# Sliding-window attention and two gated layers on one core: when q and k are loaded, and who adds the mask in the first rounds

## The chip, the cores and the metric

The kernel runs on one core of a Trainium2 chip. The metric is the device time of one execution in microseconds (us). The engines are TensorE (PE: matmuls and, as PEld, the loads of their weights), VectorE (DVE), ScalarE (ACT), GpSimd (POOL) and SyncE (SP), whose queue issues every transfer of this kernel.

## The reference

Three layers follow one another. q, k and v are (4, 8, 576, 64); the second and third layer have width 512, and inner width 1024.

```python
scores = scale * np.matmul(q, k.transpose(0, 1, 3, 2))
mask = (rel >= 0) & (rel < 64)                 # rel = query position - key position
scores = np.where(mask, scores, -1000000000.0)
attn = exp(scores - max) / (sum + 1e-09);  x = attn @ v
h = np.maximum(x @ w_in, 0.0)
conv_out = sum over k of conv_w[k] * hp[:, k:k + S, :]          # 3 taps along the sequence
x = (h * gate) @ w_out                                          # gate = 1 / (1 + exp(-conv_out))
h = np.maximum(x @ moe2_w_in, 0.0);  u, v = halves of h
v_s = einsum('ts,bsd->btd', w_spatial, layernorm(v)) + b_spatial
out = (u * v_s) @ moe2_w_out
```

## The kernel before, in words

**Attention.** The 576 positions of a batch are 9 blocks of 64. Because the window is 64 wide, a block of queries needs two blocks of keys. A round takes two blocks in turn over all batches, so there are 18 rounds (`rec_round`), and rounds 0 to 3 are of batch 0, round 4 is half of batch 0 and half of batch 1, round 9 is the first of batch 2. In a round TensorE makes scores for 8 heads in 32 small matmuls (line 537) into two PSUM tiles `s` of 4 heads each, of which the pool has two. For each head VectorE adds the mask, negates and scales, and takes the minimum in one fused pass, written to SBUF as `sm` (line 553). ScalarE takes the exponential with that minimum as bias and sums it (line 562). Then come the division (line 578 or 582), a transpose on TensorE (592), a copy (285) and the product with v (618), whose result is split into a high and a low part as `xc`, the input of the next layer.

**Loads of q, k and v.** Batch 0 is read in five tiles (`rec_load_first`, line 454) and transposed on TensorE (489). Batches 1 to 3 are read by `rec_load_qk` (line 466), eight transfers a batch (four of q, four of k) straight into `qT` and `kT` in pieces of 32 elements, and put in order by VectorE's 32x32 transpose (503). Batches 0 and 2 share one buffer, 1 and 3 the other. v comes in windows of 128 positions (`rec_load_v`, line 477) into three buffers.

**The conv layer.** x is cut into 8 chunks of 288 positions. For a chunk, `rec_g1` makes 8 column groups of h (lines 710 to 712), followed by relu, three taps and the gate on ScalarE and VectorE; `rec_g2` makes y (777 to 779) one chunk later and stores it to DRAM (802). The weights arrive as 64-bit numbers in two `raw` buffers (676 for w_in, 638 for w_out and moe2_w_in), are turned to float32 by VectorE and ScalarE (650 to 665) and split into high and low parts (`split`); all matmuls of the two gated layers are done in three such parts. The first chunk needs rounds 0 to 2, the second rounds 3 and 4.

**The last layer** begins when all chunks are done (`rec_v`, `rec_u`, `rec_sp`, `rec_o`).

**The order.** Nothing is issued in the order in which it is written down. Each step is an operation of `Plan` with a rank (its due time, from the constants in `PLAN`), its dependencies, its buffers and one planned duration per engine that may run it. `Plan.emit` plays this through with one queue per engine (T, V, A, P, D for SP): an operation becomes ready when what it depends on is done, the ready operation of lowest rank is taken when its engine is free, and the list that results is the order in which each engine gets its instructions. The times are the planner's own; on the chip an engine works through its list in order, waiting only for data and buffers. A queue with nothing more urgent that is ready takes the next ready operation at once, whatever its rank. Where several engines may run a step, each one's planned duration is multiplied by a weight (`BIAS1` before the planner's time TE1, `BIAS2` until TE2, `BIAS` after that; 1 for ScalarE).

Of the kernel before, what the change touches and what calls it, by code (L numbers as in the profile page):

```python
# [13 lines left out]
ACTF = mybir.ActivationFunctionType  # L14
ALU = mybir.AluOpType
PSUM = bass.MemoryType.PSUM
NEG = -8.0e9
BIG = 3.0e38
EXP_SHIFT = 2.0 ** -112

PLAN = {
    "BP": 2.148,
    "BP1": 0.05,
    "BP2": 15.503,
    "BV": 0.462,
    "BV1": 0.753,
    "BV2": 4.229,
    "CS": 2.842,
    "CW": 4.897,
    "CWL": -1.999,  # L30
    "DC": 1.72,
    "G2": 7.85,
    "LAT": 0.209,
    "LD": 0.07,
    "LEAD": -0.623,
    "PORT": 1.851,
    "QK": 0.74,
    "QL": -0.201,
    "QL1": -1.324,
    "QV": -0.054,  # L40
    "RD": 5.317,
    "RS": 1.023,
    "SW": 4.365,
    "TA": -1.408,
    "TE1": 1.82,
    "TE2": 574.465,
    "TL": 1.208,
    "TR": 0.83,
    "VL": -0.489,
    "W2": 13.512,  # L50
    "WI": 1.844,
    "WIS": -0.265,
    "WO": -0.591,
    "WOS": 2.232,
}
LAT = PLAN["LAT"]
HOLD, ISSUE = 0.25, 0.45
BIAS = {"V": PLAN["BV"], "P": PLAN["BP"]}
BIAS1 = {"V": PLAN["BV1"], "P": PLAN["BP1"]}
BIAS2 = {"V": PLAN["BV2"], "P": PLAN["BP2"]}  # L60
# [24 lines left out]
class Plan:  # L85
# [4 lines left out]
    def __init__(self):  # L90
        self.rows, self.bufs, self.ops = {}, [], []
        self.writer, self.readers = {}, {}
        self.port, self.issues = set(), {}

    def buf(self, key, n, make):
        return Buf(self, key, n, make)

    def op(self, rank, engs, fn, r=(), w=(), b=(), after=(), port=False, issues=1):


        i = len(self.ops)
        if port:
            self.port.add(i)
        self.issues[i] = issues
        deps = set(after)
# [12 lines left out]
        for x in b:  # L118
            x.users.append(i)
        deps.discard(i)  # L120
        self.ops.append([rank, engs, fn, deps, b])
        return i

    def emit(self):
# [18 lines left out]
        events = []  # L143
        for i in range(n):
            if not left[i]:
                heapq.heappush(events, (0.0, 0, i))
        port_free = wire = 0.0
        order = []
        t = 0.0
        while events:  # L150
            t = events[0][0]
            while events and events[0][0] <= t + 1e-9:
                _, kind, i = heapq.heappop(events)
                if kind == 0:
                    rank, opt = ops[i][0], ops[i][1]
                    e = min(
                        opt,
                        key=lambda k: (
                            max(free[k], t) + opt[k] * bias(k, t) + sum(ops[j][1][k] for r_, j in ready[k] if r_ < rank), k
                        ),  # L160
                    ) if len(opt) > 1 else next(iter(opt))
                    heapq.heappush(ready[e], (rank, i))
                elif kind == 1:
                    for j in out[i]:
                        left[j] -= 1
                        if not left[j]:
                            heapq.heappush(events, (t, 0, j))
            for e in engs:
                while ready[e] and free[e] <= t + 1e-9:
                    if e == "V" and free["P"] > t + HOLD:  # L170
# [9 lines left out]
                    if e == "V" and i in self.port:  # L180
                        begin = max(t, free["P"])
                        port_free = begin + cost
                    elif e == "P":
                        begin = max(t, port_free)
                    elif e == "D":
                        free[e] = t + ISSUE * self.issues[i]
                        wire = max(wire, free[e]) + cost
                        begin, lat = wire - cost, 2.0
                    if e != "D":
# [24 lines left out]
def tile_attention_convglu_spatial(  # L214
# [44 lines left out]
    op = plan.op  # L259
    mm = nc.tensor.matmul  # L260
    ident = const.tile([P, P], F, name="ident")
    masks = [const.tile([P, P], F, name=f"mask{j}") for j in range(3)]
# [92 lines left out]
    def setup_masks(e):  # L355


        for mk_, first in zip(masks, ((False, False), (True, False), (False, True))):
# [14 lines left out]

    op(-9.0, {"P": 0.8}, setup_ident, w=["ident"])
    op(-9.0, {"A": 1.6}, setup_table, w=["zero1"])
    op(-8.0, {"P": 3.0}, setup_masks, w=["masks"])

    def setup_ones(e):
        nc.gpsimd.memset(zero2, 0.0)
# [80 lines left out]
    def rec_load_qk(b, rank):  # L460

        for nm, src, dst in (("q", q, qT), ("k", k, kT)):
            for g in range(4):
                def ld(e, src=src, dst=dst, g=g):
                    part = src[b, 4 * (g // 2):4 * (g // 2) + 4, :, 32 * (g % 2):32 * (g % 2) + 32]
                    nc.sync.dma_start(
                        out=dst[b]()[32 * g:32 * g + 32].rearrange("p h (u c) -> p (h u) c", c=32),
                        in_=part.rearrange("h (u t) c -> t (h u) c", t=32),
                    )
                op(rank + 0.1 * g, {"D": 1.8}, ld, w=[(nm, b, "ld", g)], b=[dst[b]])  # L470

    def rec_load_v(b, w, rank):
        a = mk(at, [P, H, D], F, "vw", "vw", 3)
# [35 lines left out]
    def x_pieces(blocks):  # L509
# [9 lines left out]
            c0 += n  # L519
        return out_  # L520

    x_keys = {qc: [] for qc in range(NQ)}

    def rec_round(p, rank):
# [4 lines left out]
        sm = [mk(at, [P, HP, P], F, "sm", "sm", 4) for _ in range(2)]  # L529
        st = mk(at, [P, 3, 2, HP], F, "st", "st", 3)  # L530

        def mm_s(e):
# [9 lines left out]
        op(  # L542
            rank, {"T": 1.1}, mm_s,
            r=[("q", b, i) for b, i in blocks] + [("k", b, k0 + o) for (b, _), k0 in zip(blocks, k0s) for o in range(2)],
            w=[("s", p, h) for h in range(2)], b=pss + [qT[b] for b in bs] + [kT[b] for b in bs],
        )
        firsts = [i == 0 for _, i in blocks]
        mask = masks[1 if firsts[0] else 2 if firsts[1] else 0]
# [10 lines left out]
        def ex(h):  # L559
            def f(e):  # L560
                for hp in range(HP):
                    nc.scalar.activation(  # L562
                        out=sm[h]()[:, hp, :], in_=sm[h]()[:, hp, :], func=ACTF.Exp, scale=-1.0,
                        bias=st()[:, 0, h, hp:hp + 1], accum_out=st()[:, 1, h, hp:hp + 1],
                    )
            return f
# [25 lines left out]
                    nc.tensor.transpose(psp[h]()[:, hp, :], sm[h]()[:, hp, :], ident)  # L592
            return f
        for h in range(2):
            op(rank + 1 * rs + 0.1 * h, {"V": 1.46}, mx(h), r=[("s", p, h), "masks"], w=[("sm", p, h)], b=[pss[h], sm[h], st])
            op(rank + 2 * rs + 0.1 * h, {"A": 1.9}, ex(h), r=[("sm", p, h)], w=[("ex", p, h)], b=[sm[h], st])
# [602 lines left out]
```

## Time and profile before

| | |
|---|---|
| median of 3 runs | 548.48 us (547.16 to 550.54) |
| profiled execution | 549.49 us, span 547.7 us |
| mean granted TensorE clock | 0.956 |
| PE, PEld busy | 508.4 us (93%), 472.7 us (86%) |
| DVE, ACT, POOL busy | 345.1 us (63%), 324.4 us (59%), 4.3 us (1%) |
| transfers | 68.05 MB in 131993 packets, 105740 of them under 512 B |

Busy shares over the whole span hide that the work has stages with different limits; the rows further down are read by stretch. Matmuls overlap in their pipeline, so the mean duration of one is longer than the distance from one to the next.

### The profile page before, as it was taken

To read this page: it belongs to the slowest core of one execution; us is meant where nothing else is said; L and a number is where in the kernel's file an instruction comes from. 1 tells how busy PE (TensorE), PEld (TensorE's weight loads), DVE (VectorE), ACT (ScalarE), POOL (GpSimd) and SP (SyncE) were. 2 spreads that over 40 slices of the span, in tenths; PEclk is the share of its full clock that TensorE was granted. 3 is DMA by queue.
4 is the path that set the end of the run, shared out by engine and by line. 5 is a ranking of instruction groups with operands and counts; after the bars stand their busy time and mean duration, and the time that the engine had idled before them with its cause. 6 is when DMAs were issued, how large, how long until landed. Compare 5 with 4: busy or idle time off the path is not lost.

```text
span 547.7 us, 11063 instructions
## 1 busy us (share of the span) xinstructions
PE 508.4 (93%) x4198; PEld 472.7 (86%) x4198; DVE 345.1 (63%) x1045; ACT 324.4 (59%) x920; POOL 4.3 (1%) x34
## 2 busy tenths in 40 slices
PE   5745967999999999999999999999999999999997
PEld 5634857899988999999999998898899889988996
DVE  2547768999977989777676634986506740572160
ACT  4875879988959899678785524653322442233221
POOL 3000000000000000000000000000000000000000
PEclk9765788999998999999999999999999999999999
DMA  9999997655996746224216682560105011202003
GB/s 181 173 145 178 147 184 209 190 162 148 208 151 183 226 117 181 68 61 143 69 45 196 215 303 93 166 208 4 59 20 172 1 63 35 87 1 78 1 0 97
DMA packets 131993, 68.05 MB, mean 124 GB/s; under 512 B 105740, under 2 KB 118308, under 8 KB 131940
## 3 DMA queue, kind: packets, MB, share of 16 engines
q1 hardware_dynamic: 131940, 67.35, 51.5%
q8 instruction: 33, 0.54, 0.4%
q14 instruction: 20, 0.16, 0.1%
HBM read 48.98 MB, written 18.35 MB: 123 GB/s over the span
## 4 chain that ended last, share of the span: by engine, by line
PE 80%; DMA 7%; SPq 5%; ACT 3%; DVE 3%; issue 1%; ACTq 0%
PE y L777 6%; PE h L710 5%; PE h L711 5%; PE y L779 5%; PE h L712 5%; PE y L778 5%; DMA vw<-in_v_dram 3%; PE pv L618 3%; PE sps L1053 3%; PE sps L1055 3%; PE sps L1054 3%; PE ops L1108 3%; PE vps L930 3%; PE ops L1107 3%; PE ops L1106 3%; PE vps L929 3%
## 5 line engine op out<-in xcount | busy, mean ns | idle before, releaser
L710 PE MATMUL h<-xc,wi 128*128 128x290 f32 x256 | 79.7, 311 | 2.1 <-ACT hs L301 2.1
L777 PE MATMUL y<-g,wo 128*128 128x288 f32 x256 | 78.4, 306 | 0.8 <-DVE ys L795 0.8
L712 PE MATMUL h<-xc,wi 128*128 128x290 f32 x256 | 77.2, 301 | 0.0
L711 PE MATMUL h<-xc,wi 128*128 128x290 f32 x256 | 77.1, 301 | 0.0
L779 PE MATMUL y<-g,wo 128*128 128x288 f32 x256 | 76.1, 297 | 0.0
L778 PE MATMUL y<-g,wo 128*128 128x288 f32 x256 | 75.9, 296 | 0.0
L738 DVE SCALAR_TENSOR_TENSOR cv<-hs,cw,cv 128x288 f32<-128x288 f32 x128 | 64.5, 512 | 15.9 <-ACT cv L733 14.7
L1067 DVE TENSOR_TENSOR gr<-sps,bb 128x288 f32<-128x288 f32 x32 | 14.5, 454 | 71.9 <-PE sps L1059 71.9
L562 ACT ACTIVATE sm<-sm,st 128x128 f32<-128x128 f32 x144 | 55.7, 391 | 2.2 <-DVE st L553 2.2
L710 PEld LDWEIGHTS h<-xc,wi 128*128 128x128 f32 x256 | 49.9, 195 | 3.8 <-ACT hs L301 2.9
L777 PEld LDWEIGHTS y<-g,wo 128*128 128x128 f32 x256 | 48.5, 189 | 2.7 <-DVE ys L795 1.1
L711 PEld LDWEIGHTS h<-xc,wi 128*128 128x128 f32 x256 | 49.9, 195 | 0.0
L712 PEld LDWEIGHTS h<-xc,wi 128*128 128x128 f32 x256 | 49.6, 194 | 0.1
L779 PEld LDWEIGHTS y<-g,wo 128*128 128x128 f32 x256 | 48.7, 190 | 0.0
L778 PEld LDWEIGHTS y<-g,wo 128*128 128x128 f32 x256 | 48.6, 190 | 0.0
L578 ACT ACTIVATE sm<-sm,st 128x128 f32<-128x128 f32 x132 | 41.1, 393 | 1.0 <-DVE st L571 0.8
L285 ACT ACTIVATE gd<-gr 128x288 fp32r<-128x288 f32 (+1 forms) x32 | 13.4, 418 | 47.2 <-DVE gr L1070 47.2
L553 DVE CUSTOM_DVE_ANT_0 sm<-s,mask 128x128 f32<-128x128 f32 x144 | 32.3, 286 | 10.9 <-PE s L537 10.9
L989 PE MATMUL ups<-yt,w2i 128*128 128x288 f32 x128 | 37.9, 296 | 0.0
L990 PE MATMUL ups<-yt,w2i 128*128 128x288 f32 x128 | 37.9, 296 | 0.0
L991 PE MATMUL ups<-yt,w2i 128*128 128x288 f32 x128 | 37.9, 296 | 0.0
L618 PE MATMUL pv<-pts,vw 128*64 128x64 f32 x576 | 25.8, 250 | 12.5 <-DMA vw<-in_v_dram 9.4
(147 smaller groups left out, 1240.5 us busy)
## 6 DMA issues: line engine op xcount, KB each, us to landing
yd<-ys SPq DMA_DIRECT2D x32, 288.0 KB, 3.0
yt<-yd SPq DMA_DIRECT2D x32, 288.0 KB, 4.3
vw<-in_v_dram SPq DMA_DIRECT2D x32, 256.0 KB, 4.0
raw<-in_moe_w_out_dram SPq DMA_DIRECT2D x12, 512.0 KB, 3.9
raw<-in_moe_w_in_dram SPq DMA_DIRECT2D x16, 256.0 KB, 5.3
raw<-in_moe_w_in_dram SPq DMA_DIRECT2D x8, 512.0 KB, 5.0
w2i<-w2d SPq DMA_DIRECT2D x8, 512.0 KB, 6.1
out_dram<-osb SPq DMA_DIRECT2D x15, 256.0 KB, 2.0
```

The costliest lines, as they stand in the source:

```text
L562: nc.scalar.activation(out=sm[h]()[:, hp, :], in_=sm[h]()[:, hp, :], func=ACTF.Exp, scale=-1.0, bias=st()[:, 0, h, hp:hp + 1], accum_out=s ...
L578: nc.scalar.activation(out=sm[h]()[:, hp, :], in_=sm[h]()[:, hp, :], func=ACTF.Copy, scale=st()[:, 2, h, hp:hp + 1])
L618: mm(psv()[h * W:h * W + W, hp, j * W:j * W + W], vas[j]()[:, hp + HP * h, :], pts[h]()[:, hp, j * W:j * W + W], start=True, stop=True,)
L710: mm(hps(), wh, xh, start=(kk == 0), stop=False)
L711: mm(hps(), wh, xl, start=False, stop=False)
L712: mm(hps(), wl, xh, start=False, stop=(kk == KD - 1))
L738: return lambda e: nc.vector.scalar_tensor_tensor(out=cv(), in0=h[:, o + j:o + j + CH], scalar=cw[:, j, f:f + 1], in1=cv(), op0=ALU.mult, ...
L777: mm(yps(), wt[:, 0], gt[:, 0, :], start=(kk == 0), stop=False)
L778: mm(yps(), wt[:, 0], gt[:, 1, :], start=False, stop=False)
L779: mm(yps(), wt[:, 1], gt[:, 0, :], start=False, stop=(kk == KF - 1))
L989: mm(ups(), wt[:, 0], yt[b][0]()[:, kk, o], start=(kk == 0), stop=False)
L990: mm(ups(), wt[:, 0], yt[b][1]()[:, kk, o], start=False, stop=False)
```

## The change

It has two parts and a new set of constants.

First, `Plan.op` takes a time `at`. An operation does not become ready in the planner before it, even when all it depends on is done. Only `rec_load_qk` gives one: its own rank, which is the due time of the batch's first round less `QL`. In the same place the planner's SP queue is changed: after an issue it is not free again until the planned backlog of transfers is under `DEPTH` = 6 us, the planned issue costs 0.5 and not 0.45 us, and such a load 2.0 and not 1.8 us. No instruction of the chip is added by this; only the order of the lists changes.

Second, in rounds 0 to 5 (`EARLY = 6`) TensorE writes the mask into each of the two `s` tiles by one matmul of an identity with the mask, repeated for four heads (512 columns, float32r), and adds the scores to it. VectorE then takes one maximum over the four heads and multiplies the four results by -scale; ScalarE's exponential reads the scores from PSUM and not from `sm`, so an `s` tile stays in use until the exponential is done. For this the masks are made in a float32 tile by GpSimd and copied by VectorE into float32r tiles, with a copy of the identity; the mask's value becomes -(2 ** 33).

All but a few constants of `PLAN` change too, so that ranks, and with them the whole list, are different. By the formulas of the kernel the due time of the loads of batch 1 goes from 14.4 to 20.3 us, of batch 2 from 95.0 to 84.2, of batch 3 from 152.3 to 128.1; of the eight w_in loads from 0.4 to 18.3 before to 9.9 to 16.1; of the eight w_out loads from 25.4 to 41.1 before to 21.7 to 33.2. In `BIAS2` VectorE's weight goes from 4.229 to 4.057, GpSimd's from 15.503 to 3.837; `TE2` from 574.465 to 358.933, and beyond it VectorE's weight is 7.261 and GpSimd's 0.925.

```diff
-NEG = -8.0e9
+NEG = -(2.0 ** 33)
...
-    "BP": 2.148,
-    "BP1": 0.05,
-    "BP2": 15.503,
-    "BV": 0.462,
-    "BV1": 0.753,
-    "BV2": 4.229,
...
+    "BP": 0.925,
+    "BP1": 2.459,
+    "BP2": 3.837,
+    "BV": 7.261,
+    "BV1": 0.378,
+    "BV2": 4.057,
...
-    "QL": -0.201,
+    "QL": -1.296,
...
-    "TE2": 574.465,
+    "TE2": 358.933,
...
-HOLD, ISSUE = 0.25, 0.45
+HOLD, ISSUE, DEPTH = 0.25, 0.5, 6.0
...
-                heapq.heappush(events, (0.0, 0, i))
+                heapq.heappush(events, (max(0.0, self.at.get(i, 0.0)), 0, i))
...
-                            heapq.heappush(events, (t, 0, j))
+                            heapq.heappush(events, (max(t, self.at.get(j, 0.0)), 0, j))
...
-                        free[e] = t + ISSUE * self.issues[i]
+                        free[e] = max(t + ISSUE * self.issues[i], wire - DEPTH)
...
+    def put_masks(e):
+        for j in range(3):
+            nc.vector.tensor_copy(out=masks_r[j], in_=mf()[:, j])
+        nc.vector.tensor_copy(out=ident_r, in_=ident)
...
-                op(rank + 0.1 * g, {"D": 1.8}, ld, w=[(nm, b, "ld", g)], b=[dst[b]])
+                op(rank + 0.1 * g, {"D": 2.0}, ld, w=[(nm, b, "ld", g)], b=[dst[b]], at=rank)
...
+    EARLY = 6
...
+        early = p < EARLY
+
         def mm_s(e):
+            if early:
+                for h in range(2):
+                    mm(pss[h](), ident_r, masks_r[which].unsqueeze(1).to_broadcast([P, HP, P]), start=True, stop=False)
             for hp in range(HP):
                 for h in range(2):
                     for j, (b, i) in enumerate(blocks):
                         rows = slice(h * W, h * W + W)
                         mm(
                             pss[h]()[j * W:j * W + W, hp, :], qT[b]()[rows, hp, i * W:i * W + W],
-                            kT[b]()[rows, hp, k0s[j] * W:k0s[j] * W + P], start=True, stop=True,
+                            kT[b]()[rows, hp, k0s[j] * W:k0s[j] * W + P], start=not early,
+                            stop=not early or hp == HP - 1,
                         )
...
         def mx(h):
             def f(e):
+                if early:
+                    m = st()[:, 0, h]
+                    nc.vector.tensor_reduce(out=m, in_=pss[h](), axis=mybir.AxisListType.X, op=ALU.max)
+                    nc.vector.tensor_scalar(out=m, in0=m, scalar1=-scale, scalar2=None, op0=ALU.mult)
+                    return
...
+                    src = pss[h] if early else sm[h]
                     nc.scalar.activation(
-                        out=sm[h]()[:, hp, :], in_=sm[h]()[:, hp, :], func=ACTF.Exp, scale=-1.0,
+                        out=sm[h]()[:, hp, :], in_=src()[:, hp, :], func=ACTF.Exp, scale=scale if early else -1.0,
...
+            op(
+                rank + 2 * rs + 0.1 * h, {"A": 1.75 if early else 1.9}, ex(h),
+                r=[("sm", p, h)], w=[("ex", p, h)], b=[sm[h], st] + [pss[h]] * early,
+            )
```

## Rows read from the trace of the kernel before

**Rows 1.** Busy us (x instructions) of each engine by stretch, granted clock, DMA share

```profile
13.00:57.00 44.00, 26.13 (x287) 20.55 (x288) 25.84 (x110) 32.95 (x115) 0.00 (x0) 0.62 1.13 168
57.00:96.00 39.00, 31.25 (x319) 29.22 (x319) 30.79 (x93) 33.16 (x101) 0.00 (x0) 0.86 1.00 180
96.00:120.00 24.00, 21.91 (x204) 20.45 (x199) 23.58 (x50) 21.42 (x50) 0.00 (x0) 1.00 0.61 174
120.00:200.00 80.00, 78.05 (x829) 74.35 (x829) 69.83 (x235) 66.09 (x213) 0.00 (x0) 0.98 0.81 178
...
120.00:547.70 427.70, 421.72 (x3335) 395.59 (x3334) 261.67 (x772) 232.04 (x645) 0.00 (x0) 1.00 0.39 110
```

**Rows 2.** The chain that ended last: start us, us, what

```profile
46.68 6.63 DMA vw<-in_v_dram
...
78.58 6.65 DMA vw<-in_v_dram
```

**Rows 3.** The SP queue in order of time: start us, us, what it issued

```profile
17.66 1.41 SPq L466 DMA_DIRECT2D qT<-in_q_dram  x1
...
27.11 2.92 SPq L676 DMA_DIRECT2D raw<-in_moe_w_in_dram  x2
...
39.04 2.85 SPq L454 DMA_DIRECT2D qk<-in_q_dram  x2
...
52.34 0.60 SPq L466 DMA_DIRECT2D qT<-in_q_dram  x1
...
66.13 2.58 SPq L676 DMA_DIRECT2D raw<-in_moe_w_in_dram  x2
...
70.04 2.80 SPq L466 DMA_DIRECT2D qT<-in_q_dram  x1
...
75.72 2.17 SPq L676 DMA_DIRECT2D raw<-in_moe_w_in_dram  x2
...
97.91 7.70 SPq L638 DMA_DIRECT2D raw<-in_moe_w_out_dram  x3
...
139.79 0.41 SPq L466 DMA_DIRECT2D qT<-in_q_dram  x1
```

**Rows 4.** TensorE in order of time: scores of rounds 2, 3, 4, 9

```profile
22.19 1.10 PE L537 MATMUL s<-kT,qT 64*64 64x128 f32 x32
...
25.77 1.20 PE L537 MATMUL s<-kT,qT 64*64 64x128 f32 x32 [1.89 <-ACT kT L285]
...
47.78 1.99 PE L537 MATMUL s<-kT,qT 64*64 64x128 f32 x32
...
57.15 0.59 PE L710 MATMUL h<-xc,wi 128*128 128x290 f32 x1
...
151.58 1.10 PE L537 MATMUL s<-kT,qT 64*64 64x128 f32 x32
```

**Rows 5.** Groups by line and form, 0 to 120 us: count, busy us, mean ns

```profile
L562 ACT ACTIVATE sm<-sm,st 128x128 f32<-128x128 f32 x56 | 21.6, 392 | 1.6 <-DVE st L553 1.6
...
L710 PE MATMUL h<-xc,wi 128*128 128x290 f32 x68 | 22.6, 332 | 2.1 <-ACT hs L301 2.1
...
L553 DVE CUSTOM_DVE_ANT_0 sm<-s,mask 128x128 f32<-128x128 f32 x56 | 12.6, 286 | 7.3 <-PE s L537 7.3
...
L285 ACT ACTIVATE pts<-pt 128x512 f32<-128x512 f32 x14 | 8.4, 598 | 0.5 <-PE pt L592 0.4
...
L553 DVE DVE_READ_ACCUMULATOR2_ANT st<- 128x1 f32 x56 | 4.7, 84 | 0.0
...
L285 ACT ACTIVATE wi<-wt 128x512 fp32r<-128x512 f32 x7 | 4.4, 631 | 0.0
...
L306 DVE TENSOR_TENSOR xc<-pv,xc 128x512 fp32r<-128x512 f32 x4 | 2.7, 680 | 0.2 <-ACT xc L285 0.2
...
L570 DVE TENSOR_SCALAR st<-st 128x4 f32<-128x4 f32 x6 | 1.0, 165 | 2.2 <-ACT sm L562 2.2
...
masks.py:199 POOL TENSOR_SCALAR_AFFINE_SELECT ident<-ident 128x128 f32<-128x128 f32 x1 | 0.3, 292 | 0.1
```

More of the change, by code (lines that the diff above doesn't have):

```diff
@@ L21 @@
 PLAN = {
-    "BP": 2.148,
-    "BP1": 0.05,
-    "BP2": 15.503,
-    "BV": 0.462,
-    "BV1": 0.753,
-    "BV2": 4.229,
-    "CS": 2.842,
-    "CW": 4.897,
-    "CWL": -1.999,
+    "BP": 0.925,
[4 more added lines that the diff above has]
+    "BV2": 4.057,
+    "CS": 2.298,
+    "CW": 1.037,
+    "CWL": -1.498,
     "DC": 1.72,
-    "G2": 7.85,
+    "G2": 0.435,
     "LAT": 0.209,
[L34 to L37, printed above, removed]
-    "QL": -0.201,
[L39 to L45, printed above, removed]
-    "TE2": 574.465,
[L47 to L54, printed above, removed]
+    "LD": 2.893,
+    "LEAD": 2.263,
+    "PORT": 4.777,
+    "QK": 0.786,
+    "QL": -1.296,
+    "QL1": -1.611,
+    "QV": 1.559,
+    "RD": 1.978,
+    "RS": 1.79,
+    "SW": 0.744,
+    "TA": -1.335,
+    "TE1": 2.007,
+    "TE2": 358.933,
+    "TL": -0.795,
+    "TR": 5.148,
+    "VL": -10.672,
+    "W2": 15.278,
+    "WI": 0.476,
+    "WIS": -1.114,
+    "WO": 4.681,
+    "WOS": 1.641,
 }
 LAT = PLAN["LAT"]
-HOLD, ISSUE = 0.25, 0.45
+HOLD, ISSUE, DEPTH = 0.25, 0.5, 6.0
 BIAS = {"V": PLAN["BV"], "P": PLAN["BP"]}
@@ L92, in __init__, with op @@
         self.writer, self.readers = {}, {}
-        self.port, self.issues = set(), {}
+        self.port, self.issues, self.at = set(), {}, {}
     def buf(self, key, n, make):
         return Buf(self, key, n, make)
-    def op(self, rank, engs, fn, r=(), w=(), b=(), after=(), port=False, issues=1):
+    def op(self, rank, engs, fn, r=(), w=(), b=(), after=(), port=False, issues=1, at=0.0):
         i = len(self.ops)
@@ L104, in op @@
         self.issues[i] = issues
+        self.at[i] = at
         deps = set(after)
@@ L261, in tile_attention_convglu_spatial @@
     ident = const.tile([P, P], F, name="ident")
-    masks = [const.tile([P, P], F, name=f"mask{j}") for j in range(3)]
+    masks_r = [const.tile([P, P], R, name=f"mask{j}") for j in range(3)]
+    masks = [x_.bitcast(F) for x_ in masks_r]
+    ident_r = const.tile([P, P], R, name="ident_r")
     cw = const.tile([P, 3, KF], F, name="cw")
@@ L355, in setup_masks @@
     def setup_masks(e):
-        for mk_, first in zip(masks, ((False, False), (True, False), (False, True))):
+        for mk_, first in zip([mf()[:, j] for j in range(3)], ((False, False), (True, False), (False, True))):
             for h in range(2):
@@ L375, in tile_attention_convglu_spatial @@
     op(-9.0, {"A": 1.6}, setup_table, w=["zero1"])
-    op(-8.0, {"P": 3.0}, setup_masks, w=["masks"])
+    mf = mk(p2, [P, 3, P], F, "wu", "mf", 1)
+    def put_masks(e):
+        for j in range(3):
+            nc.vector.tensor_copy(out=masks_r[j], in_=mf()[:, j])
+        nc.vector.tensor_copy(out=ident_r, in_=ident)
+    op(-8.0, {"P": 3.0}, setup_masks, w=["masks_f"], b=[mf])
+    op(-7.0, {"V": 0.6}, put_masks, r=["masks_f", "ident"], w=["masks", "masks_r"], b=[mf])
     def setup_ones(e):
@@ L530, in rec_round @@
         st = mk(at, [P, 3, 2, HP], F, "st", "st", 3)
+        firsts = [i == 0 for _, i in blocks]
+        which = 1 if firsts[0] else 2 if firsts[1] else 0
+        mask = masks[which]
+        early = p < EARLY
         def mm_s(e):
+            if early:
+                for h in range(2):
+                    mm(pss[h](), ident_r, masks_r[which].unsqueeze(1).to_broadcast([P, HP, P]), start=True, stop=False)
             for hp in range(HP):
@@ L542, in rec_round @@
         op(
-            rank, {"T": 1.1}, mm_s,
-            r=[("q", b, i) for b, i in blocks] + [("k", b, k0 + o) for (b, _), k0 in zip(blocks, k0s) for o in range(2)],
+            rank, {"T": 1.75 if early else 1.1}, mm_s,
+            r=["masks_r"] * early + [("q", b, i) for b, i in blocks] + [("k", b, k0 + o) for (b, _), k0 in zip(blocks, k0s) for o in range(2)],
             w=[("s", p, h) for h in range(2)], b=pss + [qT[b] for b in bs] + [kT[b] for b in bs],
         )
-        firsts = [i == 0 for _, i in blocks]
-        mask = masks[1 if firsts[0] else 2 if firsts[1] else 0]
         def mx(h):
             def f(e):
+                if early:
[3 more added lines that the diff above has]
+                    return
                 for hp in range(HP):
@@ L594, in rec_round @@
         for h in range(2):
-            op(rank + 1 * rs + 0.1 * h, {"V": 1.46}, mx(h), r=[("s", p, h), "masks"], w=[("sm", p, h)], b=[pss[h], sm[h], st])
-            op(rank + 2 * rs + 0.1 * h, {"A": 1.9}, ex(h), r=[("sm", p, h)], w=[("ex", p, h)], b=[sm[h], st])
+            kept = [sm[h], st] if not early else [st]
+            op(
+                rank + 1 * rs + 0.1 * h, {"V": 0.85 if early else 1.46}, mx(h),
+                r=[("s", p, h), "masks"], w=[("sm", p, h)], b=[pss[h]] + kept,
+            )
+            op(
+                rank + 2 * rs + 0.1 * h, {"A": 1.75 if early else 1.9}, ex(h),
+                r=[("sm", p, h)], w=[("ex", p, h)], b=[sm[h], st] + [pss[h]] * early,
+            )
             if p < first_rounds:
```

## The prediction

> **What bounds the kernel now.** I read the busy time by stretch first, then the chain of work that ended last, then the queue that issues the transfers, then TensorE's order of work, then the costs by line. From 120 us to the end TensorE is busy for 421.72 of 427.70 us [rows 1]: that part is matmul, and nothing in the change makes a matmul there shorter. Before 120 us it is another kernel. TensorE is busy for 26.13 of 44, 31.25 of 39 and 21.91 of 24 us, so 27.7 us of idle time lie between 13 and 120 us, and its granted clock is 0.62 in the first of these stretches and 0.86 in the second: some of the busy time is half speed besides [rows 1]. VectorE and ScalarE are not full either: 80.2 and 87.5 us of 107. What is full is the transfer side, with a share of 1.13 and 1.00 up to 96 us and 0.61 after it [rows 1]. (A share over 1 counts packets that overlap on one engine.)
>
> The chain says the same by name: three waits for a window of v, the first and the last of them 6.6 us long, stand on it between 46 and 86 us [rows 2]. The SP queue shows why these windows are late. The eight loads of q and k of batch 1 (line 466) begin to issue at 17.66 us, and with one pair of w_in halves between them they hold the queue until 39.04 us; only then comes the last tile of batch 0, and behind it more w_in and the windows of v that the chain waits for. From 52.34 to 75.72 us the same happens with the eight loads of batch 2 [rows 3]. Who needs them? The blocks are taken two at a time, nine a batch, so batch 1 is first read by round 4, whose scores start at 47.78 us, and batch 2 by round 9, at 151.58 us: that batch is fetched 75 us too early, while the first conv matmul has waited until 57.15 us for x [rows 4].
>
> **The loads of q and k.** By the queue's own times one batch costs 39.04 - 17.66 - 2.92 = 18.5 us and the other (66.13 - 52.34) + (75.72 - 70.04) = 19.5 us [rows 3]. The change keeps a ready load out of the planner's list until its due time, and lets the planner run at most 6 us ahead of its wire. Due times follow from the constants: batch 1 at 20.3 us and batch 2 at 84.2 us, both in the planner's clock (before: 14.4 and 95.0, but only as ranks, so an idle queue took them at once). All eight w_in conversions are now due by 16.1 and the first three windows of v by 14.5. So I expect in the SP queue: the tiles of batch 0, three windows of v, three or four w_in, then batch 1 mixed with the rest of w_in, then w_out, and batch 2 only behind w_out. Batch 1 is still moved before 120 us, so its move brings the first rounds forward and saves no transfer time; batch 2's 19.5 us leave the crowded stretch altogether. The last w_out issues, at 97.91 us and 7.70 us after it [rows 3], would then come near 85 us. That is the transfer side's limit on the gain: **19.5 us**.
>
> The second limit is VectorE and ScalarE, which convert the weights, and run the softmax and the gate. Between 13 and 120 us they carry 167.7 us of work, 78% of 214; from 96 to 120 us, where no load is missing, 45.0 of 48, which is 94% [rows 1]. If the same work, less 9.2 us (next part), is packed at 94%, the 107 us become 158.5/2/0.94 = 84.3: a gain of 22.7. I don't expect that from the first us on: three rounds of attention run through both engines in turn before any conv work exists. At 86%, midway between the two, it is 158.5/2/0.86 = 92.2 us, a gain of **14.8 us**; at 80% it is 99.1, a gain of 7.9. I take 14.8, under both limits.
>
> What the move costs: batch 2 now occupies SP for its 19.5 us somewhere past 85 us, in front of stores of y, the split weights' stores and later windows of v, all on that queue. Batch 3 does exactly that in the trace, from 139.79 us [rows 3], and the stretch from 120 to 200 us around it lost 80 - 78.05 = 2 us of TensorE [rows 1]. I take **1 us**, bounds 0 and 2. The loads are not too late: round 9 is due no earlier than about 135 us in any of these cases.
>
> **Mask and maximum in rounds 0 to 5.** Removed from VectorE for each half round: four fused mask-and-minimum passes of 286 ns and their four accumulator reads of 84 ns, 1.48 us. Added: one maximum over 128x512 from PSUM and a 4-element scaling. The trace has no such maximum. The nearest row is the 128x512 subtraction that reads PSUM, 680 ns; half of it bounds it from below, four fused passes (1.14 us) from above. The scaling is the 4-element row, 165 ns [rows 5]. With 0.68 + 0.165 = 0.85 us a half round saves 0.63, twelve of them **7.6 us** of VectorE (2.1 to 11.7). ScalarE's 48 exponentials read PSUM and not SBUF: a 128x512 copy takes 598 ns from PSUM and 631 from SBUF [rows 5], so 33 ns each, **1.6 us** in all, and nothing if that does not carry over. These are the 9.2 us above; by themselves, with the loads as before, they would mostly shorten waiting.
>
> TensorE adds twelve matmuls of 512 columns. From the mean of a 290-column matmul, 332 ns with its pipeline [rows 5], one is at most 512/290 x 332 = 586 ns, 7.0 us together, and nothing where TensorE waits anyway. Its idle time in the two early stretches, 25.6 us [rows 1], covers them; I take 0, and had the cover gone by then it would be up to 7 us. The mask copies, four VectorE instructions of under 286 ns each, need nothing but the masks and so stand ahead of the first scores: 0, at most 1.1 us.
>
> A scores buffer is now held through the exponential, not only through the maximum. The next round's scores cannot start before 1.10 (scores) + 0.85 (first maximum) + 8 x 0.392 (exponentials) = 5.1 us, with the mask matmuls 5.1 to 6.3. In the trace rounds 2 and 3 start 3.58 us apart, rounds 3 and 4 22.0 us [rows 4]. So it binds only if the rounds come closer together than now; I take 0.
>
> **The reordered list.** The constants change the whole list, but from 120 us TensorE can gain or lose only the 6 us by which it is idle there [rows 1]: I take 0, bounds -3 and +3.
>
> **Sum.** The profiled execution took 549.5 us (span 547.7). 549.5 - 14.8 + 1 = 535.7. The runs' median, 548.48, is 1.0 us lower, so **535 us**; 1% of this kernel, 5.5 us, is about what a measurement can tell from no change.
>
> **Rivals.** (a) *The hold exists only in the planner's clock.* Nothing on the chip waits; if the planner runs ahead of the chip, 20.3 and 84.2 us are over before the real w_in and v are through, and the loads stand in front of them as now. For: before, the planner let batch 2 go as soon as a buffer came free, so its clock knew nothing of a full wire. Against: the new depth of 6 us ties its clock to the wire, and w_out has earlier due times than batch 2. What stays is a part of the VectorE saving, 2 to 3 us: **546**.
>
> (b) *GpSimd comes into the list.* The planner's weight on GpSimd falls from 15.503 to 3.837 while VectorE's stays near 4, so the low halves of the 16 converted weights, allowed on either, may go there once VectorE's queue is some 3 us long. The only 128-row tensor work of GpSimd in the trace takes 292 ns for 128 columns, by columns 1.17 us for 512, against 0.68 on VectorE [rows 5]. If VectorE stands still meanwhile, 16 of them lose 16 x (1.17 - 0.68) = 7.8 us, and the result is 535 + 8 = **543 to 544**. The Trainium skill ("SBUF — State Buffer", section "Who interferes with whom") speaks for this: a VectorE instruction with two SBUF inputs and a GpSimd instruction that reads SBUF share one port pair, which the first of them locks to its end. No run here shows it, since GpSimd does nothing after 13 us [rows 1].
>
> (c) *Slower: the scores buffer.* If the early rounds do come in quick succession, TensorE, which works in order, stands at each next round's scores until the eight exponentials are done: up to 6.3 - 3.6 = 2.7 us for each of six rounds, 16 us, with conv matmuls stuck behind it. It decides once rounds are asked for less than 5 to 6 us apart; only rounds 2 and 3 are that close now. With a third of the load gain left: 548.5 - 5 + 16 = **559**.
>
> (d) *More than forecast*: packing at 94% from the start, held back only by the transfers: 548.5 - 19.5, less the 3 us that the new list may gain = **526**.
>
> **How the numbers follow.** Forecast 0.66, its own range 528 to 542 (gains of 7 to 20 us); (a) 0.12, (b) 0.07, (c) 0.10, (d) 0.05. The range is 525 to 547: it takes in (a), (b) and (d), and leaves out (c) and the outer ends. Faster by over 1% (under 543): forecast and (d), 0.70. Within 1%: (a), (b), 0.18. Slower: (c) and what is left, 0.12.
>
> **What would show it.** Right: no load of batch 2 in the SP queue before the last w_out; the first conv matmul at 40 to 47 us instead of 57.15; the waits for v on the chain short or gone; the TensorE-bound part beginning near 105 us instead of 120 with its length unchanged; about 0.85 us of VectorE for each early half round. Wrong: transfers still at a share of 1 at 90 us (a), GpSimd busy between 20 and 110 us with VectorE idle beside it (b), TensorE waiting at line 537's matmuls for the exponential (c), or the part after 120 us longer by more than 3 us.

## The result and the profile after

The changed kernel takes 541.1 us (median of 4 runs, 538.86 to 541.75) against 548.3 (547.16 to 550.54): ratio 0.9856, 95% interval 0.9819 to 0.9894. Its profiled execution took 538.86 us with a span of 537.1 and is the fastest of its four, so the two profiles lie 10.6 us apart and the medians 7.2. Run again beside the experiments below it came to 0.9847 (0.9817 to 0.9877). So it is faster by 1.5%, some 8 us, where 13.5 were forecast.

The stretches that answer to [rows 1], in the same columns:

```profile
13.00:57.00 44.00, 25.66 (x272) 20.29 (x273) 26.72 (x66) 29.95 (x110) 0.00 (x0) 0.73 1.19 172
57.00:96.00 39.00, 33.34 (x367) 29.86 (x365) 36.73 (x82) 35.88 (x103) 0.00 (x0) 0.96 0.59 160
96.00:120.00 24.00, 23.25 (x222) 22.54 (x222) 21.91 (x71) 19.80 (x60) 0.00 (x0) 1.00 1.13 184
...
120.00:537.10 417.10, 412.46 (x3282) 386.70 (x3280) 250.71 (x725) 229.66 (x636) 22.84 (x26) 1.00 0.40 114
```

The first two of the three early stretches did not change alike. From 57 to 96 us the transfers' share fell from 1.00 to 0.59, and VectorE and ScalarE rose from 63.95 to 72.6 of 78 us, 93%. From 13 to 57 us they were no busier: transfers at 1.19, the two engines at 56.7 of 88 us, against 58.8 before. The second crowded stretch of transfers now lies at 96 to 120 us (1.13), where TensorE is busy for 23.25 of 24 us all the same. After 120 us TensorE idles for 4.6 us, 6.0 before. Its granted clock rose in the first two stretches, from 0.62 to 0.73 and from 0.86 to 0.96 of full speed; how much of the gain comes by way of the clock was not separated.

What TensorE does earlier is the matmuls with w_out. The first of them, before (line 777) and after (line 809):

```profile
103.81 0.38 PE L777 MATMUL y<-g,wo 128*128 128x288 f32 x1
...
87.31 0.29 PE L809 MATMUL y<-g,wo 128*128 128x288 f32 x1
```

By 120 us line 809 has run 36 times against 20 for line 777, and of the matmuls with w_in line 742 has run 70 times against 68 for line 710. Each stands for a group of three. Line 809 starts at 87.31, 87.70 and 88.10 us, 0.40 us apart, so these 18 groups are, as an estimate, 7 us of TensorE's work: the size of the gain.

The SP queue, to be held against [rows 3]:

```profile
24.64 0.60 SPq L478 DMA_DIRECT2D qT<-in_q_dram  x1
...
34.85 3.60 SPq L708 DMA_DIRECT2D raw<-in_moe_w_in_dram  x2
38.49 0.60 SPq L478 DMA_DIRECT2D qT<-in_q_dram  x1
39.14 3.34 SPq L478 DMA_DIRECT2D kT<-in_k_dram  x1
42.59 2.68 SPq L708 DMA_DIRECT2D raw<-in_moe_w_in_dram  x2
45.36 0.55 SPq L489 DMA_DIRECT2D vw<-in_v_dram  x1
45.96 0.58 SPq L478 DMA_DIRECT2D qT<-in_q_dram  x1
46.58 4.04 SPq L478 DMA_DIRECT2D kT<-in_k_dram  x1
...
81.08 8.71 SPq L670 DMA_DIRECT2D raw<-in_moe_w_out_dram  x3
...
95.00 0.43 SPq L478 DMA_DIRECT2D qT<-in_q_dram  x1
```

Batch 2 (line 478 from 95.00 us) stands behind the last w_out, which is issued by 89.8 us instead of 105.6. Batch 1 moved only from 17.66 to 24.64 us. Four of its eight loads still stand in front of the fifth w_in (34.85), six in front of the sixth (42.59) and of the window of v at 45.36. On the chain that ended last one wait for a window of v is left, and three for w_in, of 4.8 to 6.4 us, now stand on it; the wait for v and the longest of the others, to be held against [rows 2]:

```profile
45.36 5.70 DMA vw<-in_v_dram
...
55.30 6.38 DMA raw<-in_moe_w_in_dram
```

What the loads of batch 1 in front of w_in do shows in two engines in order of time, VectorE and TensorE:

```profile
43.15 0.46 DVE L422 TENSOR_SCALAR wu<-raw 128x512 uint16<-128x512 uint16 x1 [5.81 <-DMA raw<-in_moe_w_in_dram]
50.01 0.47 DVE L422 TENSOR_SCALAR wu<-raw 128x512 uint16<-128x512 uint16 x1 [4.04 <-DMA raw<-in_moe_w_in_dram]
...
44.78 1.35 PE L617 MATMUL pt<-ident,sm 128*128 128x128 f32 x4 [7.24 <-ACT sm L603]
51.11 1.76 PE L650 MATMUL pv<-pts,vw 128*64 128x64 f32 x28 [4.56 <-DMA vw<-in_v_dram]
53.26 0.61 PE L742 MATMUL h<-xc,wi 128*128 128x290 f32 x1 [0.38 <-ACT xc L290]
```

The brackets hold the idle time before an instruction and what ended it. Conversions of w_in stand in VectorE's and ScalarE's lists ahead of the last steps of rounds 2 and 3 (a copy, the divisions), so both stop, and TensorE with them, for most of 39 to 50 us. The first conv matmul comes at 53.26 us, against 57.15 [rows 4] and the 40 to 47 expected.

The second part of the change by line and form, against [rows 5]:

```profile
L587 ACT ACTIVATE sm<-s,st 128x128 f32<-128x128 f32 x48 | 17.0, 389 | 0.0
...
L587 ACT ACTIVATION_READ_ACCUMULATOR sm<-s,st 128x1 f32 x48 | 11.1, 231 | 0.0
...
L573 DVE TENSOR_REDUCE st<-s 128x4 f32<-128x512 f32 x12 | 8.2, 685 | 4.1 <-PE s L558 4.1
...
L553 PE MATMUL s<-mask,ident_r 128*128 128x512 f32 x12 | 5.5, 530 | 1.4 <-ACT sm L587 1.4
...
L574 DVE TENSOR_SCALAR st<-st 128x4 f32<-128x4 f32 x12 | 2.0, 170 | 0.4
```

By durations a half round now costs VectorE 0.685 + 0.170 = 0.855 us, as estimated. But durations overlap on this engine: the next instruction starts before the last one's record ends. What a half round takes of the engine is the distance from its first start to the start of what comes behind it. Before, the four passes; after, the maximum and the scaling:

```profile
63.42 0.29 DVE L553 CUSTOM_DVE_ANT_0 sm<-s,mask 128x128 f32<-128x128 f32 x1 [0.90 <-PE s L537]
63.63 0.28 DVE L553 CUSTOM_DVE_ANT_0 sm<-s,mask 128x128 f32<-128x128 f32 x1
...
64.27 0.94 DVE L738 SCALAR_TENSOR_TENSOR cv<-hs,cw,cv 128x288 f32<-128x288 f32 x2
```

```profile
27.95 0.68 DVE L573 TENSOR_REDUCE st<-s 128x4 f32<-128x512 f32 x1
28.66 0.17 DVE L574 TENSOR_SCALAR st<-st 128x4 f32<-128x4 f32 x1
28.74 0.68 DVE L434 SCALAR_TENSOR_TENSOR wt<-wt,wu 128x512 int32<-128x512 int32 x1
```

That is 0.85 us before, not the 1.48 that the durations add up to, and 0.79 after: some 0.05 us saved for each half round, 0.6 us for all twelve, where 7.6 were worked out. ScalarE's exponentials overlap too, so that 389 ns from PSUM against 392 from SBUF is not their pace. On the chains, 8 exponentials with their accumulator reads take 3.08 us from SBUF (before), and 4 take 1.39 us from PSUM (after):

```profile
25.72 3.08 ACT sm L562 x16
...
29.52 1.39 ACT sm L587 x8
```

That is 385 and 348 ns each: 37 ns less, 1.8 us for all 48, where 33 ns and 1.6 us were worked out. Both engines together are spared some 2.4 us, not 9.2.

### The profile page after: what moved, and what is told of

It reads as the page before. It is cut to its first block, busy times and chain, and to the rows that moved or that the text cites. A ratio compares the mean times of both kernels' runs of the same rounds, so it can differ in the third digit from the quotient of the medians.

```text
span 537.1 us, 11062 instructions
## 1 busy us (share of the span) xinstructions
PE 504.0 (94%) x4210; PEld 467.8 (87%) x4210; DVE 340.4 (63%) x957; ACT 320.5 (60%) x920; POOL 27.2 (5%) x60
## 4 chain that ended last, share of the span: by engine, by line
PE 78%; DVE 8%; DMA 7%; ACT 5%; issue 1%; SPq 0%; POOL 0%; ACTq 0%; POOLq 0%; DVEq 0%
PE y L809 5%; PE h L742 5%; PE y L811 5%; PE y L810 5%; PE h L743 5%; PE h L744 5%; PE ups L1021 3%; PE ups L1022 3%; PE ups L1023 3%; PE sps L1085 3%; PE sps L1087 3%; PE sps L1086 3%; PE ops L1140 3%; PE vps L962 3%; PE ops L1138 3%; PE ops L1139 3%
## 5 line engine op out<-in xcount | busy, mean ns | idle before, releaser
L742 PEld LDWEIGHTS h<-xc,wi 128*128 128x128 f32 x256 | 49.0, 191 | 5.4 <-ACT xc L290 2.3
L743 PEld LDWEIGHTS h<-xc,wi 128*128 128x128 f32 x256 | 49.0, 191 | 1.2 <-DVE xc L311 1.1
L744 PEld LDWEIGHTS h<-xc,wi 128*128 128x128 f32 x256 | 48.9, 191 | 0.0
L603 ACT ACTIVATE sm<-sm,st 128x128 f32<-128x128 f32 x140 | 43.4, 399 | 5.3 <-DVE st L596 5.1
L587 ACT ACTIVATE sm<-sm,st 128x128 f32<-128x128 f32 x96 | 37.2, 394 | 0.2 <-DVE st L577 0.2
L1102 POOL TENSOR_TENSOR gr<-gr,ut 128x288 f32<-128x288 f32 x24 | 20.1, 838 | 328.8 <-DMA yt<-yd 229.6
L306 ACT ACTIVATE hs<-h 128x290 f32<-128x290 f32 x55 | 22.1, 407 | 21.0 <-PE h L744 20.8
```

The lines of the kernel that those rows point to most:

```text
L587: nc.scalar.activation(out=sm[h]()[:, hp, :], in_=src()[:, hp, :], func=ACTF.Exp, scale=scale if early else -1.0, bias=st()[:, 0, h, hp:hp ...
L603: nc.scalar.activation(out=sm[h]()[:, hp, :], in_=sm[h]()[:, hp, :], func=ACTF.Copy, scale=st()[:, 2, h, hp:hp + 1])
L742: mm(hps(), wh, xh, start=(kk == 0), stop=False)
L743: mm(hps(), wh, xl, start=False, stop=False)
L744: mm(hps(), wl, xh, start=False, stop=(kk == KD - 1))
```

## The experiments

Each was run in turn with the kernel before; ratios are to it, with 95% intervals. Two kinds stand here. In some only one queue's list or one computation is edited and every other list is that of the kernel it comes from. In the others the edit goes into the planner, and all lists are new.

| run | median us | ratio | 95% interval |
|---|---|---|---|
| changed kernel again | 539.66 | 0.9847 | 0.9817 to 0.9877 |
| changed, batch 2 early in the SP list | 554.96 | 1.0115 | 1.0088 to 1.0142 |
| changed, no hold (planned anew) | 549.33 | 1.0018 | 0.9992 to 1.0043 |
| before, hold alone (planned anew) | 544.71 | 0.9923 | 0.9896 to 0.9950 |
| before, new constants alone (planned anew) | 550.72 | 1.0033 | 1.0012 to 1.0053 |
| changed, old mask in rounds 0 to 5 | 540.55 | 0.9858 | 0.9825 to 0.9891 |
| changed, batch 1 late in the SP list | 542.26 | 0.9879 | 0.9854 to 0.9904 |
| changed, batch 1 held 18 us longer (planned anew) | 542.41 | 0.9889 | 0.9864 to 0.9914 |
| before, batch 2 behind w_out in the SP list | 561.15 | 1.0215 | 1.0183 to 1.0248 |
| before, batch 2 behind moe2_w_in in the SP list | 556.10 | 1.0129 | 1.0099 to 1.0159 |
| changed, gate multiplications on VectorE | 540.61 | 0.9850 | 0.9821 to 0.9878 |
| changed, batch 1 by rows (planned anew) | 536.37 | 0.9775 | 0.9746 to 0.9803 |

**The yardstick.** The changed kernel unedited.

> The changed kernel once more, as the yardstick for the runs beside it. Every theory: 540 to 542 us, ratio to the kernel before near 0.986.

**Is the gain the hold of batch 2?** First by the SP list alone. `plan.edit` is applied to the planner's finished order; `tag` names the loads (the edit is shown cut).

```diff
+    def move(order):
+        mv = [x for x in order if tag.get(x[2]) == ("qk", 2)]
+        rest = [x for x in order if tag.get(x[2]) != ("qk", 2)]
+        k = 1 + max(n for n, x in enumerate(rest) if tag.get(x[2]) in [("s", 4)])
+        return rest[:k] + mv + rest[k:]
```

> The changed kernel; only in the SP queue's list the eight loads of batch 2 stand where a free buffer would let them go, right behind the scores of round 4; all other lists are the changed kernel's. Theory (the gain is batch 2's 19.5 us of transfers leaving the crowded stretch): most of the gain is lost, 546 to 549 us, with waits of VectorE and ScalarE for w_out between 60 and 95 us. Rival 1 (the gain is the new constants' order on the other engines) and rival 2 (the gain is the mask and the maximum): no change beyond 2 us, 539 to 543.

It is worse than expected: 15 us lost, 7 more than the change had gained. From 57 to 96 us the share of transfers is back over 1 and everything else falls; below it, what TensorE and ScalarE waited for up to 130 and 120 us (total, times, longest):

```profile
57.00:96.00 39.00, 19.81 (x224) 17.62 (x222) 21.46 (x47) 20.49 (x62) 0.00 (x0) 0.78 1.07 169
...
PE h L746 <- ACT hs L308: 16.9, 1, 16.9
...
ACT wt L292 <- DMA raw<-in_moe_w_out_dram: 16.2, 1, 16.2
```

One conversion of w_out stands in ScalarE's list where the planner thought the load done; it stops ScalarE for 16.2 us, and TensorE waits just as long for a relu behind it. So this run gives more than the price of the transfers: a list that does not expect them is stopped as a whole. The fair comparison is one in which the planner knows:

```diff
-                op(rank + 0.1 * g, {"D": 2.0}, ld, w=[(nm, b, "ld", g)], b=[dst[b]], at=rank)
+                op(rank + 0.1 * g, {"D": 2.0}, ld, w=[(nm, b, "ld", g)], b=[dst[b]])
```

> The changed kernel with the hold alone removed, and the whole list planned anew without it (the depth of 6 us, the constants and the mask matmuls stay). Theory: batch 2 goes out once its buffer is free, in front of w_out, 546 to 555 us; that the planner knows of it makes it less bad than where only the SP list was changed (555.0). Rival (the depth of the wire alone gives the queue its right order): 540 to 543.

549.3 us: without the hold (of batches 1 to 3 together) nothing is left of the gain (1.0018 against 0.9847, 1.7% or 9.4 us). Its stretches, in the columns of [rows 1]:

```profile
57.00:96.00 39.00, 32.05 (x343) 28.30 (x342) 34.67 (x82) 34.91 (x105) 0.00 (x0) 0.91 1.06 200
96.00:120.00 24.00, 19.23 (x161) 17.43 (x160) 20.38 (x64) 20.55 (x61) 0.00 (x0) 0.79 0.42 127
```

With batch 2 in the stretch from 57 to 96 us transfers are back at 1.06, and yet VectorE and ScalarE are busy for 69.6 of 78 us, 89%. The loss comes behind it. The last w_out is issued by 100.7 us instead of 89.8, and from 96 to 120 us TensorE is busy for 19.23 of 24 us, at a granted clock of 0.79; by 120 us line 809 has run 20 times, as before the change, and not 36. So what the hold gives is, above all, w_out ahead of batch 2, and not fuller engines.

The depth of the wire does not do it alone. Nor do the constants. In the next run they were set into the kernel before, with nothing else:

```diff
-PLAN = {"BP": 2.148, ...}
+PLAN = {"BP": 0.925, ...}     # the 31 new constants
```

> The kernel before with the changed kernel's constants in PLAN and nothing else: no hold, no depth of the wire, no mask matmul. Theory: the loads of batch 1 and 2 are again taken by an idle queue, so no gain, 546 to 556 us. Rival 1 (the constants make the gain): 539 to 543.

550.7 us, 0.3% slower than before. And the hold alone in the kernel before, by the added lines of `Plan.op`, the two `heappush` lines of the change, and `at=rank` on line 470:

> The kernel before with the hold alone (loads of batches 1 to 3 not ready in the planner before their due times of 14.4, 95.0 and 152.3 us), all lists planned anew, the constants and the rest those of before. Theory (the hold of batch 2 is the gain, and a list planned with it avoids the new collision): 538 to 544 us. Rival 1 (it takes the new constants or the depth of the wire as well): 546 to 552.

544.7 us: 0.8% faster, half of the gain, and 0.7 us above the range expected. Batch 2 is issued from 102.81 us there. The other half came only with the rest of the change.

**The same move in the list of before.** Batch 2 behind the last w_out, then two loads of moe2_w_in further back, by `move` as above with `[("raw", 15)]` and `[("raw", 17)]` for `[("s", 4)]`.

> The kernel before; only in the SP queue's list the eight loads of batch 2 stand behind the last load of w_out; all other lists, constants and computations are those of before. Theory (batch 2's transfers in the crowded stretch are the cost): 538 to 543 us, with w_in 6 and 7 and the windows of v landing some 15 to 20 us earlier and VectorE and ScalarE over 90% busy from 60 to 100 us. Rival 1 (the new constants' order makes the gain, and the hold is only needed for it): 546 to 549.

> The kernel before; only in the SP queue's list batch 2's eight loads stand behind the second load of moe2_w_in (two places further back than in the run that took 561 us, where these two loads stood behind batch 2 and ScalarE waited 14.7 us for them). Theory (the hold takes some 8 us out of the stretch before 100 us, and the 561 us were the new place in the queue, not a useless hold): the wait of 14.7 us is gone, 539 to 547 us. Rival (the other engines' lists of before cannot use the earlier weights): 548 to 552.

Both were slower than the kernel before, by 12 and 7 us, and both theories' numbers were missed. In the first, 57 to 96 us became what it is in the changed kernel; the loss comes right behind it. Stretches, the SP queue and ScalarE's waits up to 200 us:

```profile
57.00:96.00 39.00, 33.20 (x366) 30.23 (x365) 35.45 (x104) 37.96 (x116) 0.00 (x0) 0.95 0.56 145
96.00:120.00 24.00, 13.34 (x121) 12.56 (x119) 12.83 (x27) 9.71 (x22) 0.00 (x0) 0.90 1.29 164
...
99.74 0.42 SPq L468 DMA_DIRECT2D qT<-in_q_dram  x1
...
114.83 2.03 SPq L642 DMA_DIRECT2D raw<-in_moe_w_in_dram  x1
...
ACT wt L287 <- DMA raw<-in_moe_w_in_dram: 21.9, 5, 14.7
```

(The digit of moe2_w_in is dropped in the rows.) The eight loads hold the queue for 15 us, the first load of moe2_w_in comes behind them, and ScalarE stands 14.7 us in front of its conversion. Two places further back that wait is gone, and another takes its place, the stores of y, which are behind the loads now:

```profile
DVE ys L290 <- DMA yd<-ys: 12.0, 1, 12.0
```

So each time the loads meet a list that does not expect them. The changed kernel sends the first load of moe2_w_in (94.63 us) ahead of batch 2 and mixes the stores of y between its loads.

**What the mask and the maximum gave.** The changed kernel's order, with the old arithmetic in rounds 0 to 5 (three of the edits; the matmuls' start and stop and the exponential's scale go back too):

```diff
-            if early:                 # mask matmuls
+            if False:
...
-                if early:             # maximum over four heads
+                if False:
...
-                    src = pss[h] if early else sm[h]
+                    src = sm[h]
```

> The changed kernel's lists, but rounds 0 to 5 compute as before: no mask matmul, four fused mask-and-minimum passes with their accumulator reads per half round, the exponential from SBUF. VectorE carries 7.6 us more before 90 us, TensorE 12 matmuls less. Theory (from 57 us VectorE and ScalarE are the bound at 92 to 94% busy; before 57 us transfers are): the rounds that fall behind 57 us cost, the earlier ones don't, 2 to 5 us slower than the changed kernel, 543 to 546. Rival 2 (mask and maximum are the whole gain): 548 to 549. Rival 3 (they are hidden, since only transfers count): within 1 us, 540 to 542.

0.9858 against 0.9847: 0.6 us, with intervals of 3 thousandths on either side. The theory's 2 to 5 us did not come, and up to some 2 us cannot be told from nothing; rival 2's 7 can. Rival 3's number stands, its reason is not shown: by the starts read above there is little to hide. (The 7.6 us in this expectation are the prediction's durations again.) From 13 to 120 us VectorE and ScalarE are busy for 169.2 of 214 us in this run, 167.7 before the change, with the same arithmetic, and it is 7.7 us faster.

**Is batch 1 what keeps 39 to 50 us idle?** First its eight loads behind the sixth w_in and the fifth window of v, by `move` with `("qk", 1)` and `[("raw", 5), ("v", 0, 4)]`; then with a hold of `rank + 18.0` for batch 1 in the planner.

> The changed kernel; only in the SP queue's list the eight loads of batch 1 stand together behind the sixth w_in and the fifth window of v. Theory (the trace shows all engines waiting from 39 to 50 us for w_in 4 and 5 and a window of v, with batch 1's loads in front of them): the first conv matmul starts at 44 to 48 us instead of 53.3, but VectorE's list then waits for batch 1 near 54 us, so the end gains 0 to 4 us, 537 to 541. Rival (the stall at 39 to 50 us is what keeps the gain at half of the forecast): 533 to 536. Rival (batch 1 is needed in that place): slower, over 542.

> The changed kernel with batch 1 held 18 us longer in the planner, and all lists planned anew for it. Theory (up to 57 us it is the sum of the transfers that binds, whichever goes first; moving batch 1 only moves the waits, as in the run where VectorE then waited 9.8 us for it): first conv matmul at 44 to 49 us, end within 3 us of the changed kernel, 538 to 543. Rival (with VectorE's list adapted, the 8 us come through): 530 to 535.

The first conv matmul came at 44.79 and 44.1 us, 8 to 9 us earlier, and yet the end came no earlier (0.9879 and 0.9889). The first run ended just above its theory's range, the second within its own. The first of the two in order of time, TensorE, VectorE and ScalarE:

```profile
44.79 0.61 PE L746 MATMUL h<-xc,wi 128*128 128x290 f32 x1 [0.90 <-ACT xc L292]
...
55.25 1.30 DVE L518 STREAM_TRANSPOSE qT<-qT 128x512 f32<-128x512 f32 x2 [9.75 <-DMA qT<-in_q_dram]
...
61.80 0.70 ACT L292 ACTIVATE wt<-raw 128x512 f32<-128x512 f32 x1 [9.30 <-DMA raw<-in_moe_w_in_dram]
```

The wait of 10 us is the same; it has moved behind the first matmuls, to batch 1 itself and the seventh w_in. In the second run the stretch up to 57 us does fill:

```profile
13.00:57.00 44.00, 33.75 (x335) 28.52 (x336) 33.54 (x83) 36.47 (x122) 0.00 (x0) 0.81 0.99 166
```

TensorE is busy for 33.75 us in it instead of 25.66, VectorE and ScalarE for 80% instead of 64%. Then TensorE waits 7.3 us at a round's scores for batch 1's k, and from 57 to 96 us it is busy for 27.48 us instead of 33.34. Both runs point to the sum of the transfers up to some 60 us as what binds, whichever goes first.

**Then make the sum smaller.** Of batch 1 round 4 needs only the first of five tiles (128 positions), but must wait for all eight loads in pieces. Here it is loaded as batch 0 is, tile by tile and in whole rows, and transposed on TensorE.

```diff
+    L1 = [t_block(1, 0) - PLAN["QL"] - 2.0 + 4.0 * t for t in range(NT)]
+    for t in range(NT):
+        rec_load_first(t, L1[t], 1, L1[t])            # of batch 1, held until L1[t]
-    for b in range(1, B):
+    for b in range(2, B):
         rec_load_qk(b, t_block(b, 0) - PLAN["QL"])
...
+    for t in range(NT):
+        rec_qk_first(t, L1[t] + 3.0, 1)
```

> The changed kernel, but batch 1's q and k are loaded as batch 0's are, in five tiles of whole rows that TensorE transposes, each tile due 4 us after the one before; VectorE's ten 32x32 transposes of batch 1 are gone, ten sets of four TensorE transposes and ten copies are added; all lists planned anew. Theory (up to 57 us the sum of the transfers binds, and of batch 1 only one tile is needed by then): first conv matmul at 43 to 49 us without a wait behind it, 533 to 538 us. Rival (VectorE and ScalarE are the bound anyway, and the copies add to them): 539 to 543.

536.4 us, 0.9775: 0.7% faster than the changed kernel, and faster than either kernel.

```profile
13.00:57.00 44.00, 33.23 (x346) 26.54 (x347) 28.35 (x72) 35.00 (x118) 0.00 (x0) 0.77 1.11 205
...
48.07 0.59 PE L742 MATMUL h<-xc,wi 128*128 128x290 f32 x1
```

From 13 to 57 us the transfers carry 205 GB/s (last column) against 172, TensorE is busy for 33.23 us against 25.66, and the first conv matmul starts at 48.07 us. Two things changed at once, cheaper transfers and a round 4 that needs one tile; their shares were not separated.

**GpSimd.** The new constants gave it 24 of the last layer's 32 multiplications. Put on VectorE at the same place:

```diff
-            lambda e: (nc.gpsimd if e == "P" else nc.vector).tensor_tensor(out=gr(), in0=gr(), in1=ut[b]()[:, d, o], op=ALU.mult),
+            lambda e: nc.vector.tensor_tensor(out=gr(), in0=gr(), in1=ut[b]()[:, d, o], op=ALU.mult),
```

> The changed kernel with the same lists, but the 24 multiplications of the last layer that its constants gave to GpSimd run on VectorE at the same place. Theory (TensorE is the bound there, and VectorE is busy under 60%): within 1 us of the changed kernel, 539 to 542. Rival (GpSimd's 838 ns against some 0.4 us on VectorE lies on the way to the last matmuls): 1 to 3 us faster, 537 to 539.

0.9850 against 0.9847: no cost can be told there.

## Why the prediction was right in direction and off in size

**The step that failed** is one term: the 14.8 us, taken from packing VectorE's and ScalarE's work at 86% over the whole of 13 to 120 us, with 9.2 us of mask work taken out. It has two parts. Packing the unchanged 167.7 us at 86% gives 107 - 97.5 = 9.5 us; taking out 9.2 us gives the other 9.2/2/0.86 = 5.3.

The second part was mis-sized in its first step. The 1.48 us for each half round were added up from durations, 4 x (286 + 84) ns, of instructions that overlap; the 167.7 us they were taken from count overlapping time once (from 0 to 120 us the passes and their reads are busy for 12.7 us by that count, 17.3 by durations). By the distances between starts VectorE is spared 0.6 us and not 7.6, and ScalarE 1.8 us, so the part comes to 2.4/2/0.86 = 1.4 us. The run with the old arithmetic puts 0.6 us on it, at most some 2.

The first part agrees in number: the runs put 9.4 us on the hold (with and without it, both planned). That is partly luck. The packing did not come about: the two engines are busy for 171.0 of 214 us from 13 to 120 us, 80%, against 78% before and 79% without the hold. What changed is the order of the work in it, w_out first, and with it TensorE's first matmul with w_out, 16.5 us earlier. The two parts are measured within the changed kernel; in the kernel before the hold alone gave 4.2 us, so they do not simply add up.

**The packing is not uniform.** Up to 57 us it stayed at 64% (67% before), from 57 to 96 us it reached 93%. I had written that the first rounds run the engines in turn; what holds them is the transfers, and I had counted batch 1's move as freeing them.

**Batch 1.** "Three or four w_in, then batch 1" was right: four. (The 16.1 us given for the conversions of w_in is the due time of their last load; the last conversion is due at 19.0.) That this would bring the first conv matmul to 40 to 47 us was wrong. The two runs that did bring it to 44 us gained nothing by it, because the same transfers were then waited for a few microseconds later.

**Batch 2.** Issued behind w_out, as expected, and needed no earlier. The last w_out came by 89.8 us, near the 85 worked out. The 1 us for its new place does not show: TensorE idles less after 120 us than before. That was no general price: in lists not planned for it the same move cost 7 to 12 us net.

**The maximum, the mask matmul and the scaling** were sized right (685, 530 and 170 ns against 680, at most 586, and 165), and ScalarE's 33 ns for each exponential came as 37. What was sized wrong are the passes that they replace.

**Rivals.** (a) is out: the planner's 20.3 and 84.2 us became 24.64 and 95.00 us on the chip. (b) did not occur: GpSimd did nothing between 13 and 120 us. Its port rule shows later (below) without a cost that can be told. (c) shows with 1.42 us, one wait of a mask matmul for the exponentials:

```profile
67.43 0.51 PE L553 MATMUL s<-mask,ident_r 128*128 128x512 f32 x1 [1.42 <-ACT sm L587]
```

(d) is out, since the packing stayed at 64% up to 57 us.

**Open.** Which of the remaining edits makes the difference between 544.7 us (hold alone) and 540 was not separated: the constants need the hold, and both change every list. The depth of the wire without the hold gave nothing; with it, it was not taken out alone. The list without the hold kept the constants of the changed kernel; whether others would suit it better was not run.

## What to carry to other kernels

A transfer that is not needed yet is worth moving where it holds back one that is needed sooner, and where the stretch it enters is planned for it: engines and queues that work in order stop as a whole for one late load, so moving batch 2's eight loads back in one queue with the other lists fixed cost 7 to 12 us here, and the same move planned into all lists gained 4 to 9. Where instructions overlap, price them by the distance between starts and not by their durations: here 1.48 us of durations were 0.85 us of the engine. Estimate the gain stretch by stretch, with the limit of each, and count what the last engine has done by a given time; one packing rate over two stretches hid that the first would not move. Where moving a wait only moves it, make the transfers cheaper or need less of them instead.

## What the runs showed of the hardware

Whole rows (64 elements) against pieces of 32: with batch 1's 2.36 MB in pieces the stretch from 13 to 57 us carried 172 GB/s at a share of 1.19, with tiles of whole rows in their place 205 GB/s at 1.11. SP was not held for less time by it: batch 1's issues take 16.2 us in the changed kernel and 17.0 us by rows.

Overlap: on VectorE a fused pass of 128 columns with its accumulator read lasts 286 + 84 ns by the records, and the next one starts 0.21 us after it. On ScalarE an exponential of 128 columns with its read takes 385 ns from SBUF and 348 from PSUM, start to start, at mean durations of 392 and 389.

GpSimd's multiplication of 288 columns takes 842 ns (446 to 459 on VectorE). Beside it VectorE's subtraction of two SBUF tiles of 64 columns takes 828 ns in the median, instead of 217. The tile `gtl` in the changed kernel, then where the multiplications run on VectorE (min, median, max in ns):

```profile
L311 DVE TENSOR_TENSOR gtl<-gr,gtl x16: 217/828/834, 355.7 to 522.1; 128x64 fp32r<-128x64 f32 x16
```

```profile
L311 DVE TENSOR_TENSOR gtl<-gr,gtl x16: 215/218/221, 356.8 to 523.0; 128x64 fp32r<-128x64 f32 x16
```

By the Trainium skill ("SBUF — State Buffer", section "Who interferes with whom") an instruction on VectorE with two SBUF inputs and one on GpSimd that reads SBUF shut each other out: the one that issues second stands until the first is done. The trace agrees for 9 of these 16, with 0.6 us each; the first of the nine starts at 405.80 us, 0.07 us after GpSimd's, and ends at 406.63, 0.08 us after it. VectorE had that time to spare, and no cost shows in the total.
